# Source order on three engines, epilogues in three parts, layer norm by tiles and 128-column products in a four-layer attention kernel

## The chip, the cores and the metric

The kernel runs on one core of a Trainium2 chip. The core has a matrix engine (PE in the profile; PEld is its weight load), a vector engine (DVE), a scalar engine (ACT), a general engine (POOL), and SyncE (SP), which here issues the DMA transfers. Each engine takes its instructions strictly in the order in which the program lists them for it, and waits at an instruction until the semaphores that it needs are there. The metric is the device time of one execution in microseconds (us), as the median over several runs.

## The reference, cut to what matters

Four layers of attention with residual, S = 2048 tokens of D = 512, 32 heads of 16. Layers 0 and 2 look at a sliding window of 256 keys, layers 1 and 3 at all keys.

```python
def layer(x, wqkv, wo, window):
    n = (x - mean(x)) / sqrt(var(x) + 1e-5)
    q, k, v = split(n @ wqkv)                 # 32 heads of 16
    s = q @ k.T / 4                           # per head, 2048 x 2048
    if window: s = where(0 <= i - j < 256, s, -1e9)
    return x + softmax(s) @ v @ wo
x = layer(x, A_wqkv, A_wo, True);  x = layer(x, B_wqkv, B_wo, False)
x = layer(x, A_wqkv, A_wo, True);  x = layer(x, B_wqkv, B_wo, False)
```

## The kernel before

All work that matters is in `fast_path`; `general_path` is compiled beside it and runs only when a flag says that sums have left their range.

**Tiling.** A layer is cut into four chunks of 512 tokens (`NQ`), a chunk into eight groups of four heads (`qd`). A window layer has three steps in a group (`attn_win`), so 96 in a layer; a full layer has sixteen (`attn_full`), so 512. A step makes two score tiles (`exps`, L643: matmuls of 64 rows by 128 columns), takes their exponential on ACT (L647), in window layers cuts the edges of the window on POOL (L709, L712), and two steps later multiplies the result with the values into an accumulator in PSUM (L687 in full layers, L719 in window layers: groups of 17 columns in strips of 32, four heads side by side). Score tiles and most products share three PSUM buffers (tag `s`); in full layers the products use the accumulator `acc[1]` instead (`bank`).

**Side work.** All other work is cut into pieces and put between the steps by a planner written in Python: class `Work` is one job, class `Side` the list of jobs of a chunk, and `clock[0]` is the planner's own estimate of time. The jobs are: `T` (`transpose`, L443 on PE, copied out by ACT L446 and DVE L449), `K` and `Q` (`project`: twelve products each for four tiles, copied out by ACT L476 and DVE L478/L479, squares on ACT L482 or POOL L484), `VV` (`values`, copied out at L567/L569), `OO` (`wo`: product, then on DVE the scaling L582, the residual L583, the statistics L408/L409, and after the fourth tile the whole `norm`), `PR` (`prep`: the weights are loaded, their column maxima taken on DVE L280/L286, scales made, and the two halves of the scaled weights written by POOL L327/L331/L332), `NN` (loads tokens of layer 0, statistics, norm) and `F` (fills DRAM scratch). `mms` issues a product of K = 128 as four matmuls of 32 columns side by side (L390). `norm` (L411) makes a reciprocal root by twelve small DVE instructions (L44 to L50) and then for each of four tiles three passes over 128x512 (L419 twice, L422).

**Epilogue.** When a group's last product with the values has been issued, `epilogue` is called: DVE transposes the accumulator (L614), updates two checks (L617, L618), makes reciprocals (L620, L621), multiplies (L622), transposes back (L624), splits in two halves (L626, L627; L627 on POOL in full layers), and SP sends the result to `oh` (L631), from which `wo` reads.

**Order.** `tc.manual_schedule(engines={PE})` (L202) keeps PE's instructions in the order in which the Python program issues them. For the other engines a scheduler places each instruction by its own estimate of when the operands are ready, at build time; `tc.high_priority` around L614 moves that transpose ahead. On the chip these orders are fixed. The start (L963 to L990) prepares the weights and the first chunk one after the other; `tails` and `lasts` (L1038 to L1040) are the jobs at the end of a window layer that no attention step accompanies.

Of the kernel before, what the change touches and what calls it, by code (L numbers as in the profile page):

```python
# [188 lines left out]
def fast_path(ctx, tc, flag, a_x, a_wqkv, a_wo, b_wqkv, b_wo, out):  # L189
# [12 lines left out]
    ctx.enter_context(tc.manual_schedule(engines={mybir.EngineType.PE}))  # L202
# [4 lines left out]
    XC, XN, V, O, KM, PH = {}, {}, {}, {}, {}, {"full": False, "free": 0.0}  # L207
# [173 lines left out]
    def mms(ps, pairs, after=1.6):  # L381


        if PH["full"] and pend:
            settle()
            PH["free"] = clock[0] + 1.6
            yield 0.1
        for i, (a, b) in enumerate(pairs):
            for g in range(0, P, 32):
                nc.tensor.matmul(ps[g:g + 32], a[:, g:g + 32], b, start=(i == 0), stop=(i == len(pairs) - 1),  # L390
                                 skip_group_check=True)
# [19 lines left out]
    def norm(l, c, xs):  # L411
# [3 lines left out]
        out = []  # L415
        for i in range(4):
# [6 lines left out]
            out.append(xh)  # L423
        XNR[l, c] = clock[0] + (0 if (l, c) == (0, 1) else 9)
        return out
# [10 lines left out]
    def transpose(l, c, xns, act):  # L436
# [135 lines left out]
    def wo(l, c):  # L572
# [4 lines left out]
        for i in range(4):  # L577
# [8 lines left out]
            if i == 3:  # L586
                XN[l + 1, c] = norm(l + 1, c, xs)
# [19 lines left out]
    def epilogue(l, c, qd, a):  # L607
# [5 lines left out]
        with tc.high_priority(HEAD_START):  # L613
            nc.vector.transpose(ot.rearrange("p b r -> p (b r)"), a)  # L614
# [17 lines left out]
        if u:  # L632
            ONR[l, c, t] = clock[0] + 9


    def exps(name, kt, qt, pr, pieces):
# [11 lines left out]
        return e  # L648

# [77 lines left out]
    class Work:  # L727
# [7 lines left out]
        def ready_at(self):  # L735
# [13 lines left out]
            if self.norm and not self.begun and NB:  # L749
# [3 lines left out]
        def may_open(self):  # L753
# [3 lines left out]
                    all(("N",) + d[1:] in DONE for d in self.deps if d[0] == "T") and  # L757
# [5 lines left out]

        def advance(self):
            if self.w and not self.open:
                self.open = True
                wused.append(self)
                t = next(self.gen)
# [4 lines left out]
            if self.norm and not self.begun:  # L773
                NB.append(self.name)
            self.begun = True
            c = next(self.gen, None)
            if c is None:
                self.done, self.going = True, False
                if self.name and self.name[0] == "T":
                    NB.remove(("N",) + self.name[1:])  # L780
                if self.name:
# [6 lines left out]
    class Side:  # L788
# [12 lines left out]
        def one(self, force=False):  # L801
# [4 lines left out]
            at = [(r, i) for r, i in at if r is not None]  # L806
            now = [i for r, i in at if r <= clock[0]]
# [41 lines left out]
        def share(self):  # L849

            self.budget = min(self.budget + (self.cost - self.spent) / max(self.steps - 3 - self.k, 1), 0.9)
            self.lag = max(self.lag - 0.29, -0.3)
            while self.q and clock[0] >= PH["free"] and self.budget >= MM / 2 and (self.lag < 0.25 or self.budget > 0.6):
# [6 lines left out]
        def finish(self):  # L860
            while self.q:
                self.one(True)

    wused, NB = [], []
# [9 lines left out]
    pvq = deque()  # L874
    PT, PK, PV, PO = 2.4, 48 * MM + 0.3, 48 * MM, 48 * MM

    def attention(l, works):
# [5 lines left out]
        for t in range(NHT if l == 3 else 1):  # L883
            for c in range(NQ):
# [10 lines left out]
                for qd in qds:  # L895
# [3 lines left out]
                    for f in (attn_win if win else attn_full)(l, c, qd, *ops, a):  # L899
# [4 lines left out]
                        sd.step()  # L904
                        if win:
                            settle(False)
                    pvq[-1].append(lambda l=l, c=c, qd=qd, a=a: epilogue(l, c, qd, a))
# [8 lines left out]
    def T(l, c, act=True):  # L916
        return Work(later(lambda: transpose(l, c, XN.pop((l, c)), act)), PT, ("T", l, c), [("N", l, c)])
# [26 lines left out]
    def OO(l, c):  # L944
        return Work(later(wo, l, c), PO, ("N", l + 1, c), [("O", l, c, NHT - 1), ("P", l % 2, 3)], True)

    def NN(c, after=()):
        def gen():
# [4 lines left out]
            XN[0, c] = norm(0, c, xs)  # L953
            yield 0.0
# [14 lines left out]
    XN[0, 0] = norm(0, 0, xs)  # L969
# [4 lines left out]
    run(transpose(0, 0, XN.pop((0, 0)), True))  # L974
# [114 lines left out]
```

## Time and profile before

| | us |
|---|---|
| median of 3 runs | 2904.52 |
| lowest, highest | 2898.94, 2909.24 |
| the profiled execution, own time | 2903.81 |
| its span in the profile | 2902.1 |
| PE / ACT / DVE / POOL busy | 2688.4 / 2383.0 / 1077.5 / 621.4 |
| products with the values, layer 0 / 1 / 2 / 3 (first to last) | 102 to 555 / 613 to 1566 / 1574 to 1875 / 1941 to 2880 |

The profile gives for each engine the busy time, the idle time before an instruction and which instruction or DMA ended it. Matmul ends are modelled, so PE's idle time is best read from who waited for whom. `PEclk` is the share of PE's clock that was granted. The stages differ: in layers 1 and 3 one engine is busy without a gap, in layers 0 and 2 none is.

### The profile page before, as it was taken

How to read it: one execution, taken by the hardware profiler on the slowest of the kernel's cores; microseconds unless marked ns; L12 is line 12 of the kernel's file. 1: busy time of each engine (PE TensorE's matmuls, PEld its weight loads, DVE VectorE, ACT ScalarE, POOL GpSimd, SP SyncE). 2: the span in 40 equal slices, each digit the busy share in tenths (PEclk: the TensorE clock that was granted, in tenths of full speed). 3: DMA queues.
4: the chain of work that ended last, by engine and by line, in shares of the span. 5: the costliest groups of instructions: out<-in, count | busy, mean ns of one | idle time of the engine just before them, and what ended most of it. 6: DMA issues, size and time to landing. Idle time of an engine off the chain costs nothing.

```text
span 2902.1 us, 71222 instructions
## 1 busy us (share of the span) xinstructions
PE 2688.4 (93%) x29530; PEld 852.5 (29%) x29530; DVE 1077.5 (37%) x2273; ACT 2383.0 (82%) x2695; POOL 621.4 (21%) x1183
## 2 busy tenths in 40 slices
PE   6777889999999999999999889889999999999997
PEld 3333444432222222222223344442222222222221
DVE  7667465521213112321233677732222232222222
ACT  3444555479999999999997666549999999999996
POOL 2467465300100000010002567500000000000000
PEclk8889999999999999999999999999999999999998
DMA  6645655442222222222233555332443334333331
GB/s 207 202 161 173 205 180 159 146 139 85 96 68 97 85 67 90 92 86 70 87 98 103 184 155 157 122 120 80 122 121 105 109 108 124 108 109 112 111 98 57
DMA packets 254110, 348.15 MB, mean 120 GB/s; under 512 B 57552, under 2 KB 160464, under 8 KB 246480
## 3 DMA queue, kind: packets, MB, share of 16 engines
q1 hardware_dynamic: 253776, 343.51, 37.6%
q8 instruction: 233, 3.82, 0.5%
q14 instruction: 101, 0.83, 0.1%
HBM read 229.64 MB, written 96.99 MB: 113 GB/s over the span
## 4 chain that ended last, share of the span: by engine, by line
PE 69%; DVE 14%; ACT 8%; issue 5%; DMA 2%; POOL 1%; SPq 1%; ACTq 0%; DVEq 0%; POOLq 0%
PE acc L687 28%; PE s L643 18%; PE acc L390 8%; ACT e L647 7%; PE pv L390 3%; PE pq L390 3%; PE acc L719 3%; PE po L390 2%; DVE ot L614 2%; DVE xh L422 1%; DVE xh L419 1%; DVE xn L419 1%; DVE sp L479 1%; DVE o L624 1%; DVE hl L627 1%
## 5 line engine op out<-in xcount | busy, mean ns | idle before, releaser
L647 ACT ACTIVATE e<-s 128x1024 f32<-128x1024 f32 (+2 forms) x2432 | 2239.6, 1191 | 119.6 <-PE s L643 115.5
L687 PE MATMUL acc<-e,vt 128*17 128x512 f32 x8192 | 1078.0, 598 | 6.0 <-DVE ot L614 4.3
L643 PE MATMUL s<-qt,kt 64*128 64x512 f16 (+3 forms) x5504 | 785.3, 356 | 76.1 <-DVE sp L479 16.2
L643 PEld LDWEIGHTS <-kt 64*128 64x128 f16 x5504 | 218.6, 94 | 869.7 <-issue 835.2
L627 POOL TENSOR_TENSOR hl<-o,hl 128x512 f16<-128x512 f32 x64 | 74.3, 1160 | 1027.4 <-DVE hl L626 947.9
L614 DVE STREAM_TRANSPOSE ot<-acc 128x512 f32<-128x512 f32 x128 | 91.4, 714 | 528.6 <-PE acc L687 444.0
L712 POOL TENSOR_SCALAR_AFFINE_SELECT e<-e 128x256 f32<-128x256 f32 x512 | 231.7, 459 | 189.4 <-ACT e L647 188.7
L687 PEld LDWEIGHTS acc<-e,vt 128*17 128x17 f32 x8192 | 136.3, 95 | 353.4 <-issue 321.5
L709 POOL TENSOR_SCALAR_AFFINE_SELECT e<-e 128x256 f32<-128x256 f32 x448 | 199.3, 450 | 125.6 <-ACT e L647 123.2
L719 PE MATMUL acc<-e,vt 128*17 128x384 f32 (+2 forms) x2816 | 209.2, 401 | 17.9 <-POOL e L709 13.8
L390 PE MATMUL pq<-xc,w 128*32 128x512 f16 x3072 | 188.6, 397 | 24.0 <-DVE sp L479 16.0
L390 PEld LDWEIGHTS <-w 128*32 128x32 f16 x4608 | 137.9, 99 | 234.5 <-issue 172.0
L476 ACT ACTIVATE sp<-pq,es 128x512 f16<-128x512 f32 x64 | 44.0, 687 | 149.2 <-PE pq L390 141.3
L390 PEld LDWEIGHTS <-oh 128*32 128x32 f16 x3072 | 95.4, 98 | 154.0 <-issue 116.2
L567 ACT ACTIVATE vt<-pv 128x512 f32<-128x512 f32 x52 | 31.1, 598 | 132.8 <-PE pv L390 132.8
L390 PE MATMUL pv<-wv,xc 128*32 128x512 f16 x2304 | 133.4, 384 | 6.3 <-DVE sp L479 5.0
L478 DVE TENSOR_SCALAR sp<-acc,es 128x512 f16<-128x512 f32 x32 | 23.9, 747 | 295.0 <-PE acc L390 295.0
L390 PEld LDWEIGHTS <-xc 128*32 128x32 f16 x3072 | 98.5, 98 | 112.7 <-issue 61.7
L484 POOL TENSOR_TENSOR sq_h<-sp_h 128x512 bf16<-128x512 f16 x27 | 29.2, 1081 | 457.9 <-DVE sp_h L478 457.9
L390 PE MATMUL acc<-xc,w 128*32 128x512 f16 x1536 | 126.2, 379 | 0.4 <-DVE sp L479 0.2
L390 PE MATMUL po<-wo,oh 128*32 128x512 f16 x1776 | 106.6, 390 | 15.7 <-DMA oh<-hl 10.2
L390 PE MATMUL acc<-xc,w_h 128*32 128x512 f16 x1296 | 114.5, 379 | 2.3 <-DVE km L516 2.3
(129 smaller groups left out, 1672.3 us busy)
## 6 DMA issues: line engine op xcount, KB each, us to landing
kt<-kf SPq DMA_DIRECT2D x128, 512.0 KB
qt<-qs SPq DMA_DIRECT2D x128, 256.0 KB
xd<-x SPq DMA_DIRECT2D x96, 256.0 KB
x<-xd SPq DMA_DIRECT2D x96, 256.0 KB
w<-wd SPq DMA_DIRECT2D x22, 1024.0 KB
kt<-kw SPq DMA_DIRECT2D x64, 256.0 KB
oh<-hl SPq DMA_DIRECT2D x512, 32.0 KB
wv<-wd SPq DMA_DIRECT2D x15, 1024.0 KB
```

The source lines that it names most:

```text
L390: nc.tensor.matmul(ps[g:g + 32], a[:, g:g + 32], b, start=(i == 0), stop=(i == len(pairs) - 1), skip_group_check=True)
L419: norm1 = lambda o: nc.vector.tensor_scalar(o, xs[i], mv[:, i, 0:1], y[:, i:i + 1], op0=ALU.subtract, op1=ALU.mult)
L476: nc.scalar.activation(sp[:, 0], ps, AF.Copy, scale=e)
L567: nc.scalar.activation(vt[:, i, :, :DH], src, AF.Copy)
L614: nc.vector.transpose(ot.rearrange("p b r -> p (b r)"), a)
L627: (nc.gpsimd if l % 2 else nc.vector).tensor_tensor(hl[:, 1], o, hl[:, 0], ALU.subtract)
L643: nc.tensor.matmul(ps[:, h, s0:s0 + wd_], kt[R * h:R * h + R, pr, kc:kc + P], qt[R * h:R * h + R, pr, qc:qc + wd_], start=True, stop=True)
L647: nc.scalar.activation(e[:, :, w0:w1], ps[:, :, w0:w1], AF.Exp, scale=SCALE)
L687: nc.tensor.matmul(a[32 * h:32 * h + DH + 1, :], V[l, j // 4][:, j % 4, 4 * qd + h, :], es_[h // 2][:, h % 2, :], start=(j == 0), stop=(j ...
L709: nc.gpsimd.affine_select(v, v, pattern=[[0, 2], [-1, P]], compare_op=ALU.is_gt, fill=0.0, base=0, channel_multiplier=1)
L712: nc.gpsimd.affine_select(v, v, pattern=[[0, 2], [1, P]], compare_op=ALU.is_ge, fill=0.0, base=0, channel_multiplier=-1)
L719: nc.tensor.matmul(a[32 * h:32 * h + DH + 1, q * P:(q + nb) * P], V[l, (4 * c + j) // 4][:, j % 4, 4 * qd + h, :], es_[h // 2][:, h % 2, s ...
```

## The change

1. `manual_schedule` now names PE, ACT, DVE and POOL: these four execute in the order in which the program issues. SP is still placed by the scheduler. The `high_priority` around the transpose of the epilogue goes.
2. `epilogue` becomes a generator of three parts; the first runs where the whole ran, the others one per following step (`eps`, `epi`). `finish` and a forced `one` also run parts.
3. `norm` becomes a generator that yields after each tile with a planned wait of 1.8 us; it is a job of its own (`NO`) after `OO`, which is renamed `M`. `transpose` waits for each tile by itself. `NN` takes statistics tile by tile. A list `XT` lets only one job at a time use the tiles of x.
4. `mms` issues one matmul of 128 columns in place of four of 32, outside full layers (`PH["full"]` false). In full layers nothing changes there.
5. Limits of `share` (full layers) fall from 0.9 and 0.6 to 0.75 and 0.45; planned times after an epilogue and a norm change.

By the two kernels' instruction orders: PE's sequence of tiles in layers 0 and 2 is the same but for some jobs that shift by a few steps, and in the tail of layer 0 the four products of `VV(1, 2)` stand ahead of those of `OO(0, 3)`, where one stood before and three behind; in layers 1 and 3 the numbers of products per step are nearly the same. The number of executed instructions is the same on DVE, ACT and POOL.

```diff
-    ctx.enter_context(tc.manual_schedule(engines={mybir.EngineType.PE}))
+    ET = mybir.EngineType
+    ctx.enter_context(tc.manual_schedule(engines={ET.PE, ET.Activation, ET.DVE, ET.Pool}))
...
         for i, (a, b) in enumerate(pairs):
-            for g in range(0, P, 32):
-                nc.tensor.matmul(ps[g:g + 32], a[:, g:g + 32], b, start=(i == 0), stop=(i == len(pairs) - 1),
-                                 skip_group_check=True)
+            if PH["full"]:
+                for g in range(0, P, 32):
+                    nc.tensor.matmul(ps[g:g + 32], a[:, g:g + 32], b, start=(i == 0), stop=(i == len(pairs) - 1),
+                                     skip_group_check=True)
+            else:
+                nc.tensor.matmul(ps, a, b, start=(i == 0), stop=(i == len(pairs) - 1))
...
+        DONE["N0", l, c] = clock[0]
         for i in range(4):
...
             nc.vector.tensor_tensor(xh[:, 1], xn, xh[:, 0], ALU.subtract)
-            out.append(xh)
-        XNR[l, c] = clock[0] + (0 if (l, c) == (0, 1) else 9)
-        return out
+            XN[l, c].append(xh)
+            XNR[l, c, i] = clock[0] + (0 if (l, c) == (0, 1) else 3 if i else 5)
+            yield wait(1.8)
...
         for i in range(4):
-            yield "wait", XNR[l, c] + 2.3 * i
+            while len(xns) <= i:
+                yield wait(1.8)
+            yield "wait", XNR[l, c, i]
...
             stats(l + 1, c, i, xs[i])
-            if i == 3:
-                XN[l + 1, c] = norm(l + 1, c, xs)
+            X[l + 1, c] = xs
...
-        with tc.high_priority(HEAD_START):
-            nc.vector.transpose(ot.rearrange("p b r -> p (b r)"), a)
+        nc.vector.transpose(ot.rearrange("p b r -> p (b r)"), a)
...
         nc.vector.reciprocal(r, r)
+        yield
...
         nc.vector.transpose(o, ot.rearrange("p b r -> p (b r)"))
+        yield
...
-            ONR[l, c, t] = clock[0] + 9
+            ONR[l, c, t] = clock[0] + 5.5
...
+    def epi():
+
+        if eps:
+            if next(eps[0], "end") == "end":
+                eps.popleft()
+                epi()
...
-            self.budget = min(self.budget + (self.cost - self.spent) / max(self.steps - 3 - self.k, 1), 0.9)
+            self.budget = min(self.budget + (self.cost - self.spent) / max(self.steps - 3 - self.k, 1), 0.75)
...
                         sd.step()
+                        epi()
...
-                    pvq[-1].append(lambda l=l, c=c, qd=qd, a=a: epilogue(l, c, qd, a))
+                    pvq[-1].append(lambda l=l, c=c, qd=qd, a=a: (eps.append(epilogue(l, c, qd, a)), next(eps[-1])))
...
+    def NO(l, c):
+
+        return Work(later(lambda: norm(l, c, X.pop((l, c)))), 0.0, ("N", l, c), [("M", l, c)], aside=True)
```

More of the change, by code (lines that the diff above doesn't have):

```diff
@@ L747, in ready_at @@
                 return None
-            if self.norm and not self.begun and NB:
+            if self.norm and not self.begun and (NB or self.name[1] == 0 and XT):
                 return None
@@ L806, in one @@
             at = [(r, i) for r, i in at if r is not None]
+            if force and not at and eps:
+                epi()
+                return self.one(True)
             now = [i for r, i in at if r <= clock[0]]
@@ L952, in gen @@
                 stats(0, c, i, xs[i])
[L953 to L954 removed]
+                yield wait(0.9)
+            yield from norm(0, c, xs)
         return Work(gen(), 0.0, ("N", 0, c), after, aside=True)
```

54 lines of the change are left out of this document (33 added, 21 removed).

## The prediction

> **What bounds the kernel now.** I read the span first, then the busy time by stage, then in the stages that matter who ended PE's waits.
>
> ```profile
> span 2902.1 us, 71222 instructions
> ```
>
> ```profile
> 75.00:556.00 481.00, 393.58 (x5994) 184.94 (x5986) 298.20 (x591) 248.10 (x325) 263.48 (x549) 0.93 0.56 177
> ...
> 628.00:1502.00 874.00, 863.49 (x8136) 205.01 (x8132) 198.90 (x451) 870.08 (x943) 63.73 (x58) 1.00 0.26 85
> 1566.00:1875.00 309.00, 270.70 (x4151) 127.75 (x4147) 221.70 (x486) 201.41 (x246) 203.86 (x483) 0.95 0.51 158
> ...
> 1957.00:2860.00 903.00, 889.40 (x7889) 211.60 (x7887) 229.04 (x453) 900.84 (x983) 64.82 (x58) 1.00 0.35 107
> ```
>
> Columns of the stage rows: stretch, its length, busy time of PE, PEld, DVE, ACT and POOL with instruction counts, PE clock, DMA share, GB/s. In the full layers (628 to 1502, 1957 to 2860) ACT is busy 870.08 of 874 and 900.84 of 903 us: the exponentials set the end, and an edit that leaves ACT's work as it is gains at most 4 and 2 us there. In the window layers (75 to 556, 1566 to 1875) no engine is full: PE 394 of 481 and 271 of 309, ACT 248 and 201, DVE 298 and 222, POOL 263 and 204, and the granted clock is 0.93 and 0.95. Time can be won only there, so I ask who kept PE waiting.
>
> ```profile
> PE pq L390 <- DVE sp L479: 15.2, 5, 9.1
> PE acc L719 <- POOL e L709: 13.2, 8, 3.8
> PE s L643 <- DMA qt<-qs: 12.5, 1, 12.5
> PE s L643 <- DVE xc L449: 7.8, 7, 2.3
> PE s L643 <- DVE sp L479: 6.2, 5, 2.6
> ...
> PE acc L719 <- POOL e L712: 3.9, 2, 2.4
> ```
>
> ```profile
> PE s L643 <- DVE sp L479: 10.0, 3, 5.9
> PE pt L443 <- DVE xh L419: 7.2, 2, 3.8
> PE s L643 <- ACT e L647: 5.6, 12, 1.2
> PE pt L443 <- DVE xc L449: 4.7, 1, 4.7
> PE s L643 <- DVE dx L582: 4.4, 4, 1.3
> ```
>
> The first view is layer 0, the second layer 2 with its tail. The waits that a DVE instruction ended come to 52.5 us in the first (29.2 in the three rows shown, 23.3 in eight smaller ones) and 36.9 in the second (26.3 shown, 10.6 in eight smaller ones): 89.4 together. POOL ended 17.1 in the first. What made DVE late? Two of the longest, on its timeline:
>
> ```profile
> 314.04 1.82 DVE L280 TENSOR_SCALAR wr<-wr,upv 128x512 f32<-128x512 f32 x4 [14.13 <-DMA wr<-in_B_wo_dram]
> 315.90 3.72 DVE L286 TENSOR_REDUCE wa<-wr 128x256 f32<-128x1024 f32 x2
> ...
> 323.23 0.75 DVE L479 SCALAR_TENSOR_TENSOR sp<-pq,es,sp 128x512 f16<-128x512 f32 x1
> ```
>
> ```profile
> 1688.91 0.71 DVE L419 TENSOR_SCALAR xn<-x,mv,y 128x512 f32<-128x512 f32 x1
> ...
> 1692.38 0.89 DVE L422 TENSOR_TENSOR xh<-xn,xh 128x512 f16<-128x512 f32 x1
> ...
> 1693.28 0.74 DVE L479 SCALAR_TENSOR_TENSOR sp<-pq,es,sp 128x512 f16<-128x512 f32 x1
> ```
>
> In the first, PE waits 9.1 us for the copy at 323.23. DVE had stood 14.13 us at the head of its queue for weights, then scaled them (1.82) and reduced them (3.72): preparation that the source issues in the next chunk and the scheduler hoisted. In the second (5.9 us) the copy at 1693.28 stands behind the norm of three more tiles: from 1688.91 to 1693.27 four passes of L419 and two of L422, 4.3 us.
>
> **The change, part by part.** Sum against the profiled execution, 2903.81 us (span 2902.1 and 1.7 outside), 0.7 below the median of 2904.52.
>
> *Source order, norm by tiles, epilogue in parts.* Comparing the two instruction orders: on DVE 401 of 561 instructions in layer 0 and 204 of 488 in layer 2 move by three places or more, in the full layers 20 of some 475 each; ACT's order in the full layers is unchanged. In layer 0 a copy of a product (L479) has on average 9.2 us of DVE work moved behind it and 0.6 ahead. The hoisted 5.5 us of the first stall and the 4.3 of the second go behind the copy: 9.8 of 15.0, 65%. Smaller stalls have less of it, for an epilogue that stays ahead, or the latency through two copies, remains. Laid against the new order one by one, the DVE-ended stalls over 0.4 us lose between nothing and all; I take 45% of 89.4, **-40 us**. Ends: 11% (the two shown alone), -10; 90%, -80. What is late next where DVE is on time is the PSUM buffer that ACT empties (5.6 us in layer 2's row already).
>
> *The first queries.*
>
> ```profile
> 83.61 0.40 PE L501 MATMUL phq_None<-sq,hsum 128*32 128x512 bf16 x4
> ...
> 84.83 3.68 DVE L286 TENSOR_REDUCE wa<-wr 128x256 f32<-128x1024 f32 x2 [1.84 <-DMA wr<-in_B_wqkv_dram]
> 88.43 0.74 DVE L532 TENSOR_SCALAR m_None<-phq_None,kx 128x512 f16<-128x512 f32 x1
> ...
> 96.47 0.82 PE L643 MATMUL s<-qt,kt 64*128 64x384 f16 x4 [12.46 <-DMA qt<-qs]
> ```
>
> The sums for the first queries are done at 84.01, but DVE waits 1.84 us for weights, reduces them for 3.68, and only then writes the shifts (88.43), on whose round trip through DRAM PE waits until 96.47. In the new order nothing of that stands ahead of the shifts: **-4.4 us**, 88.43 less 84.0. Ends: 0 (the transfers decide) and -12.5 (the whole wait). The norm of chunk 1, part of which ran in gaps earlier, now follows the shifts; its four tiles, some 2 us each by the second DVE fence, lie under PE's wait for the shifts' round trip, and without that cover they cost the first transposes that much.
>
> *POOL.* Weight parts ran in one unbroken stretch:
>
> ```profile
> 158.22 1.17 POOL L332 TENSOR_TENSOR w<-wr,w 128x512 f16<-128x512 f32 x1
> ```
>
> A triple of multiply, cast and subtract is at most three such passes, 3.5 us. In the new order one or two triples stand between the cuts of a step instead of all eight in a row, but as many must be done in the same steps. I take half of 17.1 us, **-8.5**; ends +5 (the cuts behind triples in more steps) and -17.
>
> The same stretch held DVE:
>
> ```profile
> 157.72 10.59 DVE L617 TENSOR_TENSOR lmin<-lmin,ot 128x16 f32<-128x16 f32 x1
> 168.23 0.17 DVE L618 TENSOR_TENSOR lsum<-lsum,ot 128x16 f32<-128x16 f32 x1
> ```
>
> An instruction that takes 0.17 us next time took 10.59 while POOL ran without a pause. [...] If every preparation in layer 0 (three such stretches) held DVE for 10 us again where it happened once, it would be +20; I leave it out of the sum, since such a row occurs once.
>
> *Products of 128 columns.*
>
> ```profile
> 1615.43 0.84 PE L719 MATMUL acc<-e,vt 128*17 128x384 f32 x8
> 1616.20 1.07 PE L443 MATMUL pt<-ident,xh 128*128 128x128 f16 x16
> 1617.20 0.40 PE L501 MATMUL phq_None<-sq,hsum 128*32 128x512 bf16 x4
> ...
> 1621.44 0.84 PE L719 MATMUL acc<-e,vt 128*17 128x384 f32 x8
> 1622.10 2.77 PE L390 MATMUL pq<-xc,w 128*32 128x512 f16 x48
> 1624.81 0.50 PE L643 MATMUL s<-qt,kt 64*128 64x384 f16 x4
> ```
>
> Twelve products start at 1622.10 and the scores at 1624.81: 2.71 us, 0.22 each, streaming 512 columns with four strips abreast. One matmul of 128 columns streams the same 512. Its weights are four times as wide; the nearest row is the transpose, which loads 128 columns of the same type before every matmul: sixteen in 1616.20 to 1617.20, 0.06 us each, load included. A load that fits under 0.06 is hidden under 0.22: **0**. What it does cost is a change of the array's shape. From the last eight products with the values to the twelve, 1621.44 to 1622.10, is 0.66 us; from an equal eight to transposes, 1615.43 to 1616.20, is 0.77: 0.11 more, and today's products need no change after products with the values. The new order has 58 more such changes in layer 0 and 34 in layer 2; 92 by 0.11 is 10, some inside waits: **+8**, ends 0 and +10.
>
> *Tail of layer 0.*
>
> ```profile
> 562.88 8.60 PE L390 MATMUL po<-wo,oh 128*32 128x512 f16 x156 [1.78 <-DMA oh<-hl]
> ...
> 571.29 7.96 PE L390 MATMUL pv<-wv,xc 128*32 128x512 f16 x144
> ...
> 577.68 0.69 DVE L422 TENSOR_TENSOR xh<-xn,xh 128x512 f16<-128x512 f32 x1
> ...
> 579.18 0.84 PE L443 MATMUL pt<-ident,xh 128*128 128x128 f16 x12
> ```
>
> Today three value products (571.29 to 579.2) cover the norm of the last tile group, whose first tile is ready at 578.4. In the new order those products run earlier, under the last epilogue, where PE waits 1.8 us for its result today; the norm, some 7 us from the last product (571.3) to 578.4, lies open: 7.1 less 1.8, **+5**, ends 0 and +7.
>
> *Clock.* 0.93 of 481 us and 0.95 of 309 are at most 34 and 15 us of lost clock. [...]
>
> *At nothing:* fewer PE instructions (PE is paced by columns); the epilogue's later parts (the result is used a planned 5.5 us later; without that cover PE waits as it does for the 1.78 us above); the limits of `share` (the same products per step to a few); SP, which issues as many DMAs, its loads of x now waiting for single tiles of a norm, and behind them the loads of qt and kt, issued at least four steps ahead of use in both orders.
>
> Sum: -40 - 4.4 - 8.5 + 8 + 5 - 5 = -44.9, so **2859 us**.
>
> **Rivals.** *The waits only change hands:* each freed copy is followed by a PSUM buffer or cut that is late instead. Then -10 of the first term and the first queries remain, and the prices +8 and +5: 2902. For it: ACT and POOL waits stand in both views; against it, PE has idle time in plenty and ACT is busy 52% in layer 0.
>
> [...]
>
> *Slower by the weights.* If the load of 128 columns is not hidden, each of the 1896 products outside full layers pays it:
>
> ```profile
> L443 PEld LDWEIGHTS <-xh 128*128 128x128 f16 x512 | 36.8, 113 | 54.1 <-issue 33.0 <-DVE xh L422 10.3 <-DVE xh L419 9.1
> ```
>
> At the row's mean of 113 ns that is +214: 3073. It decides against the change from 45/1896, 24 ns per product. Against it stands the pace of the transposes. [...]
>
> *Slower by order.* If a full layer's accumulator is not turned at once, because DVE in source order is at two copies of 0.75 us, PE stops at each of 64 groups, and ACT's queue, with 4 us of slack in 874, runs dry: up to 0.8 by 64, +51 on 2859, 2910. It decides from 0.7 us per group. Against it: the unchanged order there.
>
> **How the numbers follow.** Forecast 0.60 (its own range 2825 to 2890), all of it 0.10, both faster. Change of hands 0.15, around 2902: 0.05 faster, 0.06 within, 0.04 slower than what this kernel's measurement can tell from no change, about 0.3% or 9 us. Weights 0.07, slower. Order 0.08: 2910 is within the 9 us, and with any other term at its bad end above it, so 0.05 within and 0.03 slower. Together faster 0.75, the same 0.11, slower 0.14. The range runs from 2815, where the first term is at -80 and the others as taken (2819) or a little better, to 2899, where little but the first queries and POOL is gained; it leaves out "all of it", the weights and the slower part of the rest.
>
> **What would show it.** Right: DVE-ended waits of PE near 50 us in the two stages in place of 89; no wait of DVE for weights inside layer 0; the first scores near 92 us; twelve products still 2.6 us apart; 0.1 us more where products follow products with the values; ACT still full in the full layers, each as long as before; layer 0 shorter by some 30 us and layer 2 by some 15. Wrong: a product pace above 0.24 us; products with the values of a full layer that last longer than now (613 to 1566, 1941 to 2880); PE waits for ACT or POOL that grow by what DVE's lose.

## The result, and the profile after

The changed kernel takes 2921.94 us (median of 5 runs, 2919.84 to 2924.23) against 2901.86 for the kernel before (5 runs): a ratio of 1.0068, 95% interval 1.0053 to 1.0083. It is slower by 20 us, where 2859 was forecast. Lines of the kernel after: L395 product of 128 columns, L392 product of 32 columns in full layers, L451 transpose, L454/L457 its copies, L484/L487 copies of a product, L651/L655 scores and exponential, L702/L734 products with the values, L724/L727 cuts, L620 to L635 epilogue, L424/L427 norm.

The stage rows of the kernel after, from 75.5 us on and cut at the last product with the values of one layer and the first of the next (columns as in the prediction). In order: layer 0, its tail, layer 1, layer 2, its tail, layer 3.

```profile
75.50:557.60 482.10, 402.04 (x3268) 165.21 (x3266) 307.23 (x621) 252.37 (x324) 268.04 (x547) 0.92 0.55 174
557.60:620.20 62.60, 52.02 (x256) 22.43 (x256) 27.51 (x61) 15.52 (x24) 0.00 (x0) 0.89 0.49 159
620.20:1576.70 956.50, 943.76 (x8940) 225.13 (x8940) 214.36 (x478) 943.72 (x1021) 70.31 (x66) 1.00 0.27 83
1576.70:1892.60 315.90, 279.43 (x2724) 113.77 (x2723) 224.82 (x486) 203.26 (x246) 205.28 (x486) 0.95 0.51 154
1892.60:1959.00 66.40, 55.50 (x276) 24.70 (x278) 25.95 (x59) 15.25 (x24) 0.01 (x1) 0.92 0.41 127
1959.00:2899.20 940.20, 924.83 (x8169) 219.01 (x8167) 234.22 (x455) 936.51 (x1021) 64.08 (x58) 1.00 0.35 105
```

Cut in the same way, the kernel before has 479.6, 57.5, 953.9, 308.1, 66.2 and 939.4. The full layers are nearly as long (+2.6 and +0.8) and the tail of layer 0 takes 5.1 more. The window layers, which were to lose 45 us between them, take 2.5 and 7.8 more. Their waits, layer 0 first and then layer 2, the longest in total of each (what PE waited for, us in total, times, longest):

```profile
PE pq L395 <- DVE sp L487: 11.7, 5, 6.1
PE acc L734 <- POOL e L724: 10.7, 8, 3.4
PE s L651 <- DVE xc L457: 10.2, 8, 2.9
PE s L651 <- ACT e L655: 8.3, 12, 1.7
PE s L651 <- DMA qt<-qs: 8.0, 1, 8.0
PE pt L451 <- DVE xh L424: 6.4, 3, 4.5
```

```profile
PE s L651 <- ACT e L655: 9.4, 17, 1.2
PE pt L451 <- DVE xh L424: 5.7, 3, 3.7
PE s L651 <- DVE xc L457: 5.2, 5, 3.0
PE s L651 <- DVE sp L487: 5.0, 3, 2.4
```

With the smaller rows, waits that DVE ended fall from 52.5 to 46.3 in layer 0 and from 30.0 to 22.5 in layer 2 (without its tail): 13.7 us gained. Waits that ACT ended rise from 2.6 to 12.5 and from 7.0 to 10.8: 13.7 lost. POOL's and the DMA's fall by 10 in layer 0. So PE waits less in both layers together, and the loss there is in its busy time, which is 9 us longer in each (393.1 to 402.0, 269.8 to 279.4) for the same columns. In layer 0 the slow clock makes up nearly all of it, in layer 2 it does not (both below). DVE's own work is hardly longer: 224.8 us in layer 2 in place of 221.3.

What one late copy costs beside its wait, on the timeline of DVE and then in stage rows of 3.41 us:

```profile
147.18 1.47 DVE L424 TENSOR_SCALAR xn<-x,mv,y 128x512 f32<-128x512 f32 x1
148.57 0.83 DVE L424 TENSOR_SCALAR xh<-x,mv,y 128x512 f16<-128x512 f32 x1
149.43 1.53 DVE L427 TENSOR_TENSOR xh<-xn,xh 128x512 f16<-128x512 f32 x1
150.88 0.62 DVE L629 TENSOR_TENSOR ot<-ot,r 128x256 f32<-128x256 f32 x1
151.53 0.71 DVE L631 STREAM_TRANSPOSE o<-ot 128x512 f32<-128x512 f32 x1
152.17 0.60 DVE L424 TENSOR_SCALAR xn<-x,mv,y 128x512 f32<-128x512 f32 x1
152.69 1.48 DVE L424 TENSOR_SCALAR xh<-x,mv,y 128x512 f16<-128x512 f32 x1
154.20 0.98 DVE L427 TENSOR_TENSOR xh<-xn,xh 128x512 f16<-128x512 f32 x1
155.10 0.74 DVE L487 SCALAR_TENSOR_TENSOR sp<-pq,es,sp 128x512 f16<-128x512 f32 x1
```

```profile
147.58:150.99 3.41, 1.56 (x20) 0.65 (x20) 3.38 (x4) 1.89 (x4) 3.27 (x4) 1.00 0.30 85
150.99:154.40 3.41, 0.00 (x0) 0.00 (x0) 3.34 (x5) 0.00 (x0) 3.35 (x6) 0.50 0.00 0
154.40:157.82 3.42, 1.92 (x5) 0.71 (x5) 3.38 (x4) 0.00 (x0) 3.28 (x4) 0.50 0.21 77
157.82:161.23 3.41, 3.41 (x10) 1.04 (x10) 3.38 (x5) 0.02 (x1) 3.33 (x4) 0.50 0.11 24
161.23:164.64 3.41, 2.41 (x22) 0.90 (x21) 3.31 (x10) 3.13 (x4) 1.13 (x4) 1.00 0.46 124
```

DVE waits for no weights here. The copy of a product that PE finished at 145.7 stands in source order behind two norm tiles and a part of the epilogue, and runs at 155.10. PE waits 6.1 us for it, until 155.90. It then works for 5.3 us (1.92 and 3.41) at a granted clock of 0.50: the twelve products from 155.90 on take 5.28 us, where twelve take 2.76 at 1.00 (1601.74, shown further below), so the slow clock costs another 2.5. Elsewhere such a wait comes back under ACT's name:

```profile
119.48 3.75 DVE L287 TENSOR_REDUCE wa<-wr 128x256 f32<-128x1024 f32 x2
...
123.98 0.75 DVE L487 SCALAR_TENSOR_TENSOR sp<-pq,es,sp 128x512 f16<-128x512 f32 x1
...
124.78 0.61 PE L651 MATMUL s<-qt,kt 64*128 64x384 f16 x4 [1.06 <-DVE sp L487]
...
125.49 1.02 ACT L655 ACTIVATE e<-s 128x1024 f32<-128x1024 f32 x1 [4.62 <-PE s L651]
...
126.57 0.61 PE L651 MATMUL s<-qt,kt 64*128 64x384 f16 x4 [1.17 <-ACT e L655]
```

The late copy ends at 124.73, the scores that wait for its PSUM buffer start, ACT (idle for 4.62 us) takes the exponential, and only when that ends, at 126.51, does the next score tile start. The 1.17 us stand under ACT, which was not late.

### The profile page after: what moved, and what is told of

The parts are those of the page before. It is cut to its first block, busy times and chain, and to the rows that moved or that the text cites. A ratio compares the mean times of both kernels' runs of the same rounds, so it can differ in the third digit from the quotient of the medians.

```text
span 2922.5 us, 59858 instructions
## 1 busy us (share of the span) xinstructions
PE 2710.3 (93%) x23842; PEld 797.3 (27%) x23842; DVE 1087.4 (37%) x2273; ACT 2390.4 (82%) x2695; POOL 627.2 (21%) x1183
## 3 DMA queue, kind: packets, MB, share of 16 engines
q1 hardware_dynamic: 253776, 343.51, 37.8%
## 4 chain that ended last, share of the span: by engine, by line
PE 70%; DVE 11%; ACT 8%; issue 5%; POOL 2%; DMA 1%; SPq 1%; ACTq 0%; DVEq 0%; POOLq 0%
PE acc L702 28%; PE s L651 18%; PE acc L392 8%; ACT e L655 7%; PE pq L395 4%; PE pv L395 4%; PE acc L734 4%; PE po L395 3%; DVE ot L620 1%; DVE xh L427 1%; DVE xn L424 1%; DVE xh L424 1%; POOL e L727 1%; DVE sp L487 1%; DMA oh<-hl 1%
## 5 line engine op out<-in xcount | busy, mean ns | idle before, releaser
L655 ACT ACTIVATE e<-s 128x1024 f32<-128x1024 f32 (+2 forms) x2432 | 2234.9, 1186 | 135.0 <-PE s L651 129.3
L702 PE MATMUL acc<-e,vt 128*17 128x512 f32 x8192 | 1079.2, 599 | 6.7 <-DVE ot L620 5.0
L651 PE MATMUL s<-qt,kt 64*128 64x512 f16 (+3 forms) x5504 | 790.0, 357 | 77.8 <-ACT e L655 19.8
L651 PEld LDWEIGHTS <-kt 64*128 64x128 f16 x5504 | 217.4, 94 | 874.8 <-issue 831.4
L620 DVE STREAM_TRANSPOSE ot<-acc 128x512 f32<-128x512 f32 x128 | 91.1, 712 | 524.9 <-PE acc L702 442.9
L727 POOL TENSOR_SCALAR_AFFINE_SELECT e<-e 128x256 f32<-128x256 f32 x512 | 236.5, 469 | 220.0 <-ACT e L655 218.8
L635 POOL TENSOR_TENSOR hl<-o,hl 128x512 f16<-128x512 f32 x64 | 74.5, 1164 | 969.5 <-DVE hl L634 888.2
L702 PEld LDWEIGHTS acc<-e,vt 128*17 128x17 f32 x8192 | 136.4, 95 | 356.2 <-issue 323.7
L734 PE MATMUL acc<-e,vt 128*17 128x384 f32 (+2 forms) x2816 | 216.4, 408 | 13.6 <-POOL e L724 11.8
L724 POOL TENSOR_SCALAR_AFFINE_SELECT e<-e 128x256 f32<-128x256 f32 x448 | 197.8, 448 | 133.5 <-ACT e L655 130.1
L395 PE MATMUL pq<-xc,w 128*128 128x512 f16 x768 | 186.0, 396 | 18.0 <-DVE sp L487 13.0
L484 ACT ACTIVATE sp<-pq,es 128x512 f16<-128x512 f32 x64 | 44.0, 687 | 133.0 <-PE pq L395 128.5
L395 PE MATMUL pv<-wv,xc 128*128 128x512 f16 x576 | 131.6, 383 | 1.0 <-ACT e L655 1.0
L492 POOL TENSOR_TENSOR sq<-sp 128x512 bf16<-128x512 f16 x32 | 33.3, 1041 | 437.4 <-DVE sp L486 437.4
L392 PE MATMUL acc<-xc,w 128*32 128x512 f16 x1536 | 126.2, 379 | 0.4 <-DVE sp L487 0.2
L392 PE MATMUL acc<-xc,w_h 128*32 128x512 f16 x1296 | 114.5, 379 | 2.3 <-DVE km L524 2.3
L395 PE MATMUL po<-wo,oh 128*128 128x512 f16 x444 | 104.2, 388 | 8.8 <-DMA oh<-hl 8.4
L395 PEld LDWEIGHTS <-w 128*128 128x128 f16 x768 | 76.0, 101 | 125.3 <-issue 52.5
L609 DVE TENSOR_TENSOR dx<-acc,gcol 128x512 f32<-128x512 f32 x60 | 41.5, 692 | 178.8 <-PE acc L392 178.8
```

What stands on the lines that cost most here:

```text
L395: nc.tensor.matmul(ps, a, b, start=(i == 0), stop=(i == len(pairs) - 1))
L492: nc.gpsimd.tensor_tensor(sq, sp[:, 0], sp[:, 0], ALU.mult)
L635: (nc.gpsimd if l % 2 else nc.vector).tensor_tensor(hl[:, 1], o, hl[:, 0], ALU.subtract)
L651: nc.tensor.matmul(ps[:, h, s0:s0 + wd_], kt[R * h:R * h + R, pr, kc:kc + P], qt[R * h:R * h + R, pr, qc:qc + wd_], start=True, stop=True)
L655: nc.scalar.activation(e[:, :, w0:w1], ps[:, :, w0:w1], AF.Exp, scale=SCALE)
L702: nc.tensor.matmul(a[32 * h:32 * h + DH + 1, :], V[l, j // 4][:, j % 4, 4 * qd + h, :], es_[h // 2][:, h % 2, :], start=(j == 0), stop=(j ...
```

## The experiments

The kernel before ran beside each set; its median lay between 2900.5 and 2904.9, so the ratios are the safer numbers. Stage lengths and waits are those of the profiled execution, which need not be the median one: it took 2924 us for the kernel after (median 2922), 2898 for a_dve_sched (2901), 2955 for b_dve_source (2968) and 2875 for a_tail (2870).

### Which engine's source order

```diff
 kernel before:  manual_schedule(engines={PE})
+b_source:       manual_schedule(engines={PE, Activation, DVE, Pool})
+b_dve_source:   manual_schedule(engines={PE, DVE})
 kernel after:   manual_schedule(engines={PE, Activation, DVE, Pool})
+a_all_sched:    manual_schedule(engines={PE})
+a_dve_sched:    manual_schedule(engines={PE, Activation, Pool})
+a_act_sched:    manual_schedule(engines={PE, DVE, Pool})
+a_pool_sched:   manual_schedule(engines={PE, Activation, DVE})
```

> The kernel before with ACT, DVE and POOL in source order and nothing else (the epilogue and the layer norm still whole). Theory (source order frees copies behind hoisted preparation but puts whole epilogues and norms ahead of copies, and ACT's copies ahead of exponentials): no gain, 2900 to 2925, with waits ended by DVE in the window layers about as before and those ended by ACT some 10 us more. Rival (source order is good by itself and parts 3 to 5 of the change spoil it): 20 us or more faster than before, under 2882.

**Measured** 2961.4 us, ratio 1.0198 (1.0184 to 1.0212). The 40 us were to come from source order together with the cut epilogue and norm; source order by itself costs 58. Layer 0 takes 499.7 us (before 479.6), layer 2 320.6 (308.1), the full layers 964.4 and 949.7 (953.9 and 939.4). Waits that DVE ended in layer 0 do not stay as expected, they rise from 52.5 to 72.1; those that ACT ended rise by 13 (2.6 to 15.8), about as expected. The longest, on DVE's timeline (the product ended on PE at 286.0):

```profile
286.06 0.59 DVE L419 TENSOR_SCALAR xn<-x,mv,y 128x512 f32<-128x512 f32 x1
...
296.56 0.77 DVE L422 TENSOR_TENSOR xh<-xn,xh 128x512 f16<-128x512 f32 x1
297.25 1.40 DVE L479 SCALAR_TENSOR_TENSOR sp<-pq,es,sp 128x512 f16<-128x512 f32 x2
```

The whole norm, four tiles, is one block in the source and therefore one block on DVE: 11.2 us ahead of a copy for which PE waits 11.6. A scheduler may cut such a block; source order cannot.

> The kernel before with DVE alone in source order; ACT and POOL stay with the scheduler. All three in source order cost 58 us. Theory (DVE carries about two thirds, as in the changed kernel, where giving DVE back to the scheduler gained 21 of 32): 2935 to 2950, the full layers some 10 us longer each, layer 0 some 15. Rival (the order of the three engines only hurts together): 2915 or less.

**Measured** 2967.9 us (2955.1 to 2970.0), ratio 1.0229 (1.0213 to 1.0245), at least as much as all three engines. On the kernel before, DVE's order carries the whole loss, not two thirds.

> The changed kernel with only PE in source order; ACT, DVE and POOL placed by the scheduler as before, the epilogue in parts, the norm by tiles and the products of 128 columns kept. Theory (source order is worth little either way; the loss lies in the other parts): within 10 us of the changed kernel. Rival (source order is the loss): back to the time before plus the shape changes, 2905 to 2912 or less. If source order is the gain that the other parts hide: slower than the changed kernel by 20 us or more, over 2940.

**Measured** 2889.7 us, ratio 0.9956 (0.9942 to 0.9969). The rival holds, and more: without source order the other parts of the change gain 13 us.

> The changed kernel with DVE alone placed by the scheduler again; PE, ACT and POOL in source order. All three placed by it gave 2890. Theory (the loss of 32 us is DVE's: in source order a copy of a product stands behind every epilogue part and norm tile issued before it): 2895 to 2903, with waits ended by DVE in layer 0 at 40 us or less in place of 46. Rival (it is ACT's, whose copies stand ahead of exponentials): 2912 or more.

**Measured** 2901.0 us, ratio 0.9999 (0.9990 to 1.0008): 21 of the 32 us, as the theory had it. What was to show it failed, though. Waits that DVE ended in layer 0 are 46.9 us, no fewer than the 46.3; those that ACT ended are 2.0 in place of 12.5, with ACT still in source order:

```profile
PE s L651 <- ACT e L655: 2.0, 5, 0.6
```

```profile
75.50:545.30 469.80, 395.22 (x3267) 162.95 (x3266) 281.57 (x585) 251.16 (x324) 261.49 (x547) 0.94 0.57 180
1564.20:1867.70 303.50, 270.33 (x2728) 112.39 (x2725) 219.08 (x485) 202.39 (x246) 204.97 (x486) 0.97 0.52 160
```

The clock rises from 0.92 to 0.94 and from 0.95 to 0.97. PE's waits fall by only 4.8 and 2.4 us in the two layers (78.9 to 74.1, 34.4 to 32.0), its busy time by 7 and 9. So most of what DVE's order costs here is not in any wait that DVE ended, but in waits under ACT's name and in the slow clock.

> The changed kernel with ACT alone placed by the scheduler again. Theory (DVE carries most of the loss, ACT the 8 us by which waits ended by ACT grew in layer 0 and 3 in layer 2): 2910 to 2916, with such waits in layer 0 at some 5 us in place of 12.5. Rival (ACT carries it all): 2895 or less.

**Measured** 2914.6 us, ratio 1.0038 (1.0024 to 1.0051). The size is right, but not what was to show it: waits that ACT ended in layer 0 are still 10.0 us.

> The changed kernel with POOL alone placed by the scheduler again. Theory (POOL's order matters little): 2919 to 2925, waits ended by POOL in layer 0 within 3 us of 12.1. Rival (cuts behind weight parts are part of the loss): 2915 or less.

**Measured** 2917.0 us, ratio 1.0048 (1.0034 to 1.0062): between theory and rival. It is 5 us less than the changed kernel, but the intervals overlap, so a loss by POOL's order is not shown. The three engines' shares by medians, 21, 7 and 5, add up to 33 for 32; each is uncertain by several us, so only DVE's is clear and the close sum is luck.

### Products of 128 columns

```diff
-            for g in range(0, P, 32):  ... matmul(ps[g:g + 32], a[:, g:g + 32], b)
+            nc.tensor.matmul(ps, a, b)     # outside full layers
```

The edit stands on the kernel before (b_mm128), on b_source (b_mm128_source), and taken back in the kernel after (a_mm32) and in a_all_sched (a_all_sched_mm32); b_mm64 has two matmuls of 64 columns on the kernel before.

> The changed kernel with products outside full layers as four matmuls of 32 columns again; all else stays. Theory (part of the 20 us is the change of the array's shape, 0.1 us for each of 92 more changes, and the slow clock that these little gaps bring): about 10 us faster than the changed kernel, 2912, with layer 0 shorter by 6 and layer 2 by 4. Rival (the shape changes lie inside waits; the loss comes from the order alone): within 3 us of the changed kernel, 2919 to 2925.

> The kernel before with ACT, DVE and POOL in source order and with products of 128 columns: against the kernel in source order alone (2961) only PE's matmuls differ, the order of ACT, DVE and POOL is the same. Theory (the 21 us that 128 columns gained on the kernel before came through the order that the scheduler chose): 2956 to 2968. Rival (128 columns are faster on PE itself): 2940, 20 us under 2961.

**Measured** 2919.2 us, ratio 1.0057 (1.0043 to 1.0070), where the kernel after has 1.0068; and 2959.2, ratio 1.0188 (1.0174 to 1.0202), where b_source has 1.0198. In both pairs ACT, DVE and POOL keep their order (in the traces all of their 6151 instructions but one on DVE), and the intervals overlap: the time shows nothing that the width of the products is worth by itself. For a_mm32 the rival holds. The stages moved otherwise than its theory said, layer 0 2.1 us longer and layer 2 9.9 shorter; the changed kernel's layer 2 has a stall of 4.4 us that this run lacks (last section).

> The kernel before with only the products of 128 columns outside full layers. Theory (shape changes cost 0.1 us each where they don't lie inside a wait): 8 us slower than before, 2910. Rival (they lie inside waits): within 3 us of before. A third, that fewer and wider matmuls lower the granted clock by themselves: over 15 us slower, with a clock in layer 0 below 0.92.

**Measured** 2881.7 us, ratio 0.9926 (0.9913 to 0.9940), which none of the three expected: 21 us faster. The stage rows of layers 0 and 2:

```profile
75.50:534.10 458.60, 395.67 (x3268) 164.34 (x3266) 291.29 (x586) 248.06 (x324) 262.90 (x547) 0.93 0.58 184
1546.10:1852.10 306.00, 273.89 (x2728) 114.00 (x2725) 220.50 (x485) 201.24 (x246) 201.57 (x483) 0.95 0.51 159
```

Layer 0 is 21 us shorter although PE is busy for 2.6 us more; PE's waits for DVE are 37.8 us there in place of 52.5, for POOL 11.8 in place of 17.1. With the pairs of fixed order this leaves the order, and the traces bear it out: of DVE's 2273 instructions some 120 stand at another place than in the kernel before, of POOL's 1183 some 30, of ACT's none.

> The changed kernel with only PE in source order and with products of 32 columns, so that only the epilogue in parts, the norm by tiles and the planned times are left of the change. Theory (products of 128 columns gain 20 us not on PE but through the order that the scheduler chooses once it counts one matmul in place of four): about 20 us slower than the same with 128 columns, 2905 to 2915. Rival (the gain of 20 us is special to the kernel before): within 5 us of 2890.

> The kernel before with products outside full layers as two matmuls of 64 columns in place of four of 32. In a fixed order the width of the products made no difference (2959 against 2961, 2922 against 2919). Theory (the gain of 128 columns comes through the scheduler, which sees fewer instructions per product): between the two, 2885 to 2900. Rival (the gain is the luck of one order): any other place, above 2905 or below 2880.

**Measured** 2905.2 us, ratio 1.0020 (1.0009 to 1.0030), 15 us slower than with 128 columns; and 2893.6, ratio 0.9971 (0.9960 to 0.9983), between four matmuls and one. Both fit. Why the scheduler does better is not shown; that its estimate counts the four matmuls one after the other would explain it, but is argued only (in the traces they do run abreast: 48 of 32 columns take 2.77 us in the kernel before, twelve of 128 take 2.76 in the kernel after).

### Epilogue and norm

```diff
+a_epi_whole, a_all_epi_whole:
-  pvq[-1].append(lambda ...: (eps.append(epilogue(l, c, qd, a)), next(eps[-1])))
+  pvq[-1].append(lambda ...: run(epilogue(l, c, qd, a)))
-  ONR[l, c, t] = clock[0] + 5.5
+  ONR[l, c, t] = clock[0] + 9
+a_norm_whole, a_all_norm_whole:
-            XNR[l, c, i] = clock[0] + (0 if (l, c) == (0, 1) else 3 if i else 5)
-            yield wait(1.8)
+            XNR[l, c, i] = clock[0] + (0 if (l, c) == (0, 1) else 9) + 2.3 * i
+        yield 0.0
+a_aside_late: the loop over aside jobs in Side.step runs behind the products
+a_all_...: also manual_schedule(engines={PE})
+a_all_epi_whole: also tc.high_priority(HEAD_START) around the epilogue's first transpose, as before
```

> The changed kernel, all engines in source order, with the epilogue whole. Theory (the epilogue in parts is what gave back the 8 to 10 us that each full layer lost in source order, and cost the 5 us of layer 0's tail): layers 1 and 3 some 964 and 950 us, tail of layer 0 58 to 60, 2932 to 2942. Rival (the parts matter only in the window layers): layers 1 and 3 as now, 956 and 940.

**Measured** 2965.2 us, ratio 1.0208 (1.0194 to 1.0222): 43 us slower than the changed kernel, more than expected. Layers 0 to 3 take 500.4, 961.1, 324.0 and 951.3 us. The epilogue in parts, with its planned time, is what repairs most of the loss of source order. The tail of layer 0 stays at 62.9, where 58 to 60 was expected, so the parts did not lengthen it.

> The changed kernel, all engines in source order, with the norm whole. Theory (the norm by tiles cost 6 us in source order with the epilogue whole): 2912 to 2920, the tail of layer 0 5 us shorter only if it, and not the epilogue in parts, lengthened that tail. Rival (with the epilogue in parts the norm by tiles gains, since its tiles then alternate with copies): 2928 or more.

**Measured** 2919.7 us, ratio 1.0066 (1.0049 to 1.0083): with the epilogue in parts the norm by tiles makes no difference that can be told. The tail of layer 0 is 64.3, so the norm by tiles does not lengthen it either.

> The changed kernel, all engines in source order, with the pieces of norm and weight preparation of a step issued behind the step's products in place of ahead of them, so that a product's copy has at most the last step's pieces ahead. Theory (copies of products stand behind norm tiles in source order): 2910 to 2916, with waits of PE ended by DVE in layer 0 at 40 us or less in place of 46. Rival (what is lost is DVE's wait at the head of its queue, whatever stands behind it): within 4 us of 2922.

**Measured** 2925.9 us (2916.7 to 2927.7), ratio 1.0071 (1.0057 to 1.0084). The rival's number holds: a new order within a step moves little. That what stands ahead of a copy was issued steps before would explain it, but is argued only.

> The changed kernel with ACT, DVE and POOL placed by the scheduler and the epilogue whole, its first transpose moved ahead as before: the kernel before plus products of 128 columns, the norm by tiles and the planned times. Theory (under the scheduler the epilogue in parts costs the 5 us of layer 0's tail and 2 us in layer 3, the norm by tiles gains 3 us in layer 2): tail of layer 0 58 us, 2877 to 2883. Rival (the norm by tiles lengthens that tail): tail 63, 2885 or more.

> The changed kernel with only PE in source order and the norm whole: the kernel before plus products of 128 columns, the epilogue in parts and the planned times. Theory (under the scheduler the norm by tiles cost 14 us, 2882 to 2896, and the epilogue in parts gained 6, 2896 to 2890): 2872 to 2880, faster than all kernels so far. Rival (the two don't add): 2882 to 2892.

**Measured** 2896.0 us, ratio 0.9970 (0.9959 to 0.9982), with a tail of 63.7: slower than b_mm128 by 14, a miss; that the tail is long goes with the rival, that the norm makes it so does not: the tail is 64.3 in a_norm_whole and 63.9 in a_all_norm_whole. And 2883.1, ratio 0.9938 (0.9925 to 0.9950), as fast as b_mm128: under the scheduler the norm by tiles costs 7 us and the epilogue in parts gains 6. With the norm whole the same parts gain nothing (2883.1 against 2881.7 of b_mm128). The sum that was to be faster than all others was not; the parts do not add.

### The tail of layer 0

```diff
 a_tail, on a_all_norm_whole
-        yield wait(8)                    # in wo
+        yield wait(0 if (l, c) == (0, 3) else 8)
-            ONR[l, c, t] = clock[0] + 5.5
+            ONR[l, c, t] = clock[0] + (2.5 if (l, c) == (0, 3) else 5.5)
             while self.q:                # in finish
-                epi()
+                while eps:
+                    epi()
                 self.one(True)
```

> The kernel of the run before (only PE in source order, products of 128 columns, epilogue in parts, norm whole: 2883, tail of layer 0 63.9 us) with the planned times of the last group of layer 0 shortened, so that in the tail the output products run behind one value product, as in the kernel before, and three value products cover the norm. Theory (the tail's 5 us come from the four value products that run ahead, and not from the norm or the epilogue): tail 57 to 59, 2876 to 2880. Rival (the tail is as long whichever product runs first): tail 62 or more, 2882 or more.

**Measured** 2869.9 us, ratio 0.9899 (0.9883 to 0.9914), the fastest kernel here: 31 us under the kernel before and 52 under the changed one, and faster than theory or rival had it. The tail of layer 0 takes 61.2 us, a miss: PE waits 2.2 us for the norm (8.2 with the other order) but 3.5 for the epilogue's transfer. The largest gain that the stages show came where it was not sought: the tail of layer 2 falls from 65.8 to 56.5. Of the three edits only the one in `finish` is not tied to layer 0. PE in that tail after the change (first fence) and in this run (second):

```profile
1892.57 20.89 PE L395 MATMUL pv<-wv,xc 128*128 128x512 f16 x96
1913.30 10.52 PE L395 MATMUL po<-wo,oh 128*128 128x512 f16 x48
1929.69 1.33 PE L451 MATMUL pt<-ident,xh 128*128 128x128 f16 x8 [5.87 <-DVE xh L424]
```

```profile
1854.77 10.53 PE L395 MATMUL pv<-wv,xc 128*128 128x512 f16 x48
1865.14 10.52 PE L395 MATMUL po<-wo,oh 128*128 128x512 f16 x48
1875.50 10.52 PE L395 MATMUL pv<-wv,xc 128*128 128x512 f16 x48
...
1888.86 0.62 PE L451 MATMUL pt<-ident,xh 128*128 128x128 f16 x8
```

```profile
1854.80:1911.30 56.50, 53.19 (x273) 23.78 (x271) 26.66 (x60) 15.08 (x24) 0.00 (x0) 1.00 0.49 150
```

In the changed kernel all eight value products (12 matmuls each) run ahead of the four output products, and the norm lies open behind these; a_all_norm_whole has the same order and waits 3.96 us there. In a_tail four of the eight run behind them, the norm is covered, and the clock stays at 1.00 (last fence) in place of 0.92.

## Why the prediction was wrong, by its own steps

**Source order, -40.** This step failed. It took 45% of the 89 us of DVE-ended waits as gone, because in two stalls the hoisted work would "go behind the copy", and because by a count more work moves behind a copy than ahead of it (9.2 us and 0.6 on average). It priced a position in the queue as time, and its count compared the kernel before with the changed one, in which the epilogue is already cut. In place of a gain, source order alone costs 58 us (b_source): it ties each copy to every block issued before it, a whole norm or epilogue among them, however late DVE is. The epilogue in parts gives back 43. Within the finished change source order still costs 32, of which DVE's is 21. The kernel with all of the change but the wide products (a_mm32) is 16 us slower than before, where the sum without its +8 has 53 less.

What the step read of the two stalls came true. In layer 0 DVE waits 1.3 us at most for the raw weights of a preparation (14.13 before), and the longest wait of PE for a product's copy falls from 9.1 to 6.1 there and from 5.9 to 2.4 in layer 2. But a list of stalls of one order does not contain those of the other: DVE-ended waits of the two layers, with the tail of layer 2, fell from 89 to 75.5, not to 50.

**Rivals.** "The waits only change hands" came about for DVE and ACT, 13.7 us each way; that it fits to the tenth is luck, and its time, 2902, is 20 us too low: PE's busy time grew by 18 us in the two layers, where the rival has +8. That ACT was late is wrong too, as a_dve_sched shows: most of the waits under ACT leave when DVE's order does. "Slower by order" has its mechanism in b_source, where each full layer lost 10 us; in layer 1 one accumulator waited 7.0 us for DVE, but in layer 3 it is the squares of a product that come late:

```profile
PE acc L687 <- DVE ot L614: 9.4, 5, 7.0
PE acc L501 <- POOL sq_h L484: 9.3, 11, 2.1
```

So five groups were hit and not all 64. In the changed kernel the epilogue in parts keeps these layers within 3 us. The rival was dismissed with "the unchanged order there", an order that the cut epilogue gave, not source order.

**First queries, -4.4.** Right, with some luck in the number: the first scores start at 88.98 (96.47 before). 3.3 of the 7.5 us go to transposes of chunk 1, which now stand behind them, so the first product with the values comes 4.2 earlier. The step named that price without putting it in the sum.

**POOL, -8.5.** PE's waits for POOL in layer 0 fell by 5.0, within the ends. A gain in time is not to be seen: with POOL back under the scheduler the kernel is, if anything, 5 us faster (a_pool_sched), and PE waits 8.9 us for POOL in place of 12.1. That every preparation holds DVE for 10 us, left out at +20, did not come about: the kernel after has one such row, of 3.63 us (last section). The row that the step set beside the 10.59 us of L617 is of L618, but the median of L617 too is 0.19 us.

**128 columns.** The pace holds, and so does the extra time ahead of the products:

```profile
1600.96 0.84 PE L734 MATMUL acc<-e,vt 128*17 128x384 f32 x8
1601.74 2.76 PE L395 MATMUL po<-wo,oh 128*128 128x512 f16 x12
```

Twelve products take 2.76 us, where they took 2.77 with 32 columns, so nothing of the wide weight load shows in the pace and the rival by the weights is out; 0.78 us pass from eight products with the values to them, 0.12 more than before. That it is the array's shape that takes this time is the author's reading. In PE's work the price is there: with what ran at a clock of 0.50 counted half, PE's busy time in layer 2 is 263.3 us with 32 columns and 266.5 with 128 (a_mm32 and the changed kernel), 259.4 and 262.9 in the other pair. That is an estimate of 3.2 and 3.5 us, where 34 changes at 0.11 make 3.7. Yet +8 in the time is not seen in either pair of fixed order. What the step missed is that the scheduler reacts to the number of matmuls: -21 us on the kernel before. With DVE and POOL in source order the change has no part in that gain.

**Tail of layer 0, +5.** Right, 62.6 against 57.5, with PE's wait of 5.9 us for the norm. Its cause held as well in layer 2 (a_tail). In layer 0 the restored order took the wait for the norm away, but PE met a transfer instead.

**Clock, -5.** No run shows this term, an estimate of the author, and its sign is wrong: the clock fell from 0.93 to 0.92 in layer 0 and from 0.97 to 0.89 in its tail, and stayed at 0.95 in layer 2. The longest waits did get shorter (in layer 0 from 12.5 and 9.1 us to 8.0 and 6.1). But the trace has 0.50 for 81.9 us of layer 0 in place of 64.9, and PE worked for 59.0 of these in place of 42.5. At half pace (5.28 us for twelve products in place of 2.76, as above) that is worth 8 us by estimate, nearly all of the 9 by which its busy time grew there. Behind which steps it fell is told in the last section. In layer 2 it was at 0.50 for 30.7 us in both; there some 3 of the 9 us go with the wide products, and the rest is not traced to a cause.

Together: -4 at the start, +7 in layer 0 after it, +5 in its tail, +3 and +1 in the full layers, +8 in layer 2.

## What to carry to other kernels

Before an engine's scheduler is switched off, look for the blocks in the source that are longer than the slack of what is issued behind them (here 11 us of norm ahead of a copy of 0.7), and cut these first; an order moved instruction by instruction says nothing of time until it is run. Price a stall with the slow clock behind it (here 2.5 us behind a wait of 6.1), and small gaps close together like one long gap (here the clock fell behind a step of 3.41 us in which PE was busy for 1.56), and follow a wait to the instruction that was late, not to the one that ended last. An edit to one engine's instructions also feeds the scheduler of the others: test it once with the order fixed and once with it free.

## What the runs showed of the hardware

**Where the clock fell.** In these traces the granted clock is 1.00 or 0.50 and changes only at whole steps of 3.41 us. In the changed kernel, from 60 us on, it fell 21 times, each time behind a step in which PE was busy for 0.47 or less; at 0.48 and above it never did. It came back only behind a step that was busy for 0.81 or more. The kernel before has 19 falls, behind steps of up to 0.41, and the clock stayed behind one of 0.45. In the nineteen kernels the bounds are less sharp: it fell at up to 0.57 and stayed at down to 0.42. So a wait need not be long. In the rows of the late copy the clock fell at 150.99, when PE had been idle for 1.2 us, with shorter gaps in the same step (busy 1.56 of 3.41). Of the 396 falls in the nineteen kernels, only 107 stood behind a gap of 3.4 us or more (5 of the 21 in the changed kernel).

**DVE held by POOL.** Instructions of DVE that otherwise take 0.2 to 0.4 us (median of the same instruction) took many times that while POOL ran without a gap. In a_all_sched, DVE and then POOL at that time:

```profile
247.63 9.06 DVE L623 TENSOR_TENSOR lmin<-lmin,ot 128x16 f32<-128x16 f32 x1
```

```profile
246.91 1.27 POOL L328 TENSOR_TENSOR wr<-wr,wd 128x512 f32<-128x512 f32 x1
...
256.05 0.61 POOL L332 CAST w<-wr 128x512 f16<-128x512 f32 x1
256.74 1.16 POOL L333 TENSOR_TENSOR w<-wr,w 128x512 f16<-128x512 f32 x1
```

In the kernel after it is a cast of the epilogue in layer 2:

```profile
1657.62 3.63 DVE L634 CAST hl<-o 128x512 f16<-128x512 f32 x1 [4.44 <-DMA oh<-hl]
```

In the nineteen kernels there are ten rows more than 2 us above that median, in nine kernels, of 3.4 to 10.6 us. All ended at POOL's first pause, here the 0.08 us between 256.66 and 256.74. The row of the kernel after, with the 4.44 us for which the cast had waited for a transfer, cost PE 4.4. Not every instruction of DVE is held: in the kernel before the transpose just ahead of the row of 10.59 us (from 156.97 on) took 0.72 us, as it does in the median, while POOL ran without a gap too. What sets the two apart stays open.
